# Delta rule and maxout layer on one core: y to DRAM in four transfers, PSUM in two pools, two steps moved

## The chip, the cores and the metric

The kernel runs on one core of one Trainium2 chip. Its time is the device time of one execution, in microseconds (us). TensorE (PE) multiplies matrices and writes to PSUM only; VectorE (DVE), ScalarE (ACT) and GpSimd (POOL) do the elementwise work; SyncE (SP) issues most of the DMA transfers. Each engine takes its own instructions in order, and an engine waits for another one by semaphores.

## The reference

Two layers follow each other. The first is a delta rule over a sequence: for each of 4 batches and 8 heads, with 768 steps of 48 dimensions, in float32. The second is a maxout layer over the 3072 rows that come out of it.

```python
k_n = k / (np.linalg.norm(k, axis=-1, keepdims=True) + 1e-06)
state = 0                                  # (B, H, 48, 48)
for t in range(768):
    y[:, :, t] = einsum('bhd,bhde->bhe', q[:, :, t], state)
    v_old = einsum('bhde,bhd->bhe', state, k_n[:, :, t])
    state += beta_t * einsum('bhd,bhe->bhde', k_n[:, :, t], v[:, :, t] - v_old)
x = y.transpose(0, 2, 1, 3).reshape(3072, 384)
h = maximum(maximum(x @ w1, x @ w2), x @ w3)      # 384 -> 768
out = h @ w_out                                    # 768 -> 384
```

## The kernel before

The sequence is cut into 12 chunks of 64 steps. A chunk is held as two units `g` of two batches each, on 128 partitions. Two chunks of all four batches make a group: 6 groups of 512 rows. For each group the recurrence makes x (in the kernel `xt`, with dimensions on the partitions), and the maxout layer of that group, the generator `ffn(m)`, runs on TensorE while VectorE and ScalarE prepare the recurrence of group m + 1. The order is written out by hand: `ffn(m)` yields after each product of a block, and after the i-th yield the table `LINKS` (or `FOURTH_LINKS` for m = 3 and `LAST_LINKS` for m = 4) names the steps of the next group that are issued there. `STEPS` says how many steps of the triangular solve follow. Within an engine the instructions stand in that order.

The steps that the change and the prediction speak of, by the letters of the tables:

- `g` (`gram`): k k' and k q' of a chunk's batches into `p_g`. DVE masks the q part (`pt`, L401), ACT copies the k part (`at`, L434), and SP sends `at` to DRAM (`at_d`, L447), four transfers for each of two units.
- `blocks`: reads them back as blocks (`x_bl`, L494). `solve` begins with a root on ACT (L272), some small DVE work (L273 to L549), and then 31 steps of two DVE instructions each (L563, L567). Its result goes through DRAM (`y_d`) into `ut`.
- `k`, `q`, `u`, `s`, `y`: products with the state (`p_k`, `p_q`), the solved values (`p_u`), the new state (`p_s`), the result y (`p_y`, added on DVE at L817).
- `x`, `w`, `X`: `y_blocks` (L853) sends y to DRAM (`y_x`), `read_y` (L864) reads it back in another order into `qall`, and `turn_y` (L875) transposes it in 32 x 32 blocks on DVE into `xt`.
- `V` loads values, and `P`, `p` (`prep_values`) scale them: from chunk 10 on DVE, L298.
- `K` loads keys of later units.

In `ffn`, `hidden` multiplies a block of 128 columns of a weight with `xt` into `p_h` (L1221, three matmuls, each shown as two). From m = 1 on, w2 - w1 and w3 - w1 stand in place of w2 and w3: the first gets a relu on ACT (L1231), the second a maximum on DVE (L1235), and what w1 gives is added behind, through w1 times w_out.

The output products of the groups m = 3 to 5 (`outputs`, L988) are done with seven products of halves in place of eight, and the hidden products of m = 5 too (`crossed_hidden`, L1164, six units of eight PSUM tiles each). The sums and differences of the weights that this needs are made by `cross_weights` (parts 0 to 2) and `cross_hidden`; those of x and h by DVE (L1017, L1144 to L1147).

PSUM has eight banks. The pool "psum" holds `ps_ffn` (two banks, in rotation: `p_h`, `p_o`) and `ps_two` (three pairs of banks: all else). At m = 5 this pool is closed, and a new one "banks" is opened, in which `ps_ffn` rotates through all eight banks; two tiles "later" are taken first. A new pool's tile waits for the last reader of what lay there. Where a tile of a rotation is asked for again, its first matmul waits for the reader of the one that had the place.

```python
        if m >= GROUPS - 1:
            psum_pool("banks")

            for _ in range(2):
                ps_ffn([128, TOK], "later")
            yield from crossed_hidden(m, hs)
```

Of the kernel before, what the change touches and what calls it, by code (L numbers as in the profile page):

```python
# [9 lines left out]
FP32 = mybir.dt.float32  # L10
# [13 lines left out]
def kernel(  # L24
# [41 lines left out]
    GROUPS = UNITS // 4  # L66
    TOK = 512
# [5 lines left out]
    dram = ctx.enter_context(  # L73
        tc.tile_pool(name="dram", bufs=2, space=bass.MemoryType.DRAM)
    )
    banks = ctx.enter_context(ExitStack())
    pools = []

    def psum_pool(name):
        banks.close()  # L80
        pools.append(
            banks.enter_context(
                tc.tile_pool(name=name, bufs=1, space=bass.MemoryType.PSUM)
            )
        )

    psum_pool("psum")

    def ps_ffn(shape, name):

        one = len(pools) > 1
        return pools[-1].tile(shape, FP32, name=name, tag="ffn", bufs=8 if one else 2)

    def ps_two(name):
        return pools[-1].tile([128, 2, 512], FP32, name=name, tag="two", bufs=3)


    kpad = [const.tile([128, H, DP], FP32, name=f"kpad{i}") for i in range(4)]
# [21 lines left out]
    def rows(bb):  # L120
        return slice(C * bb, C * (bb + 1))
# [70 lines left out]
    for bb in range(2):  # L192
        nc.gpsimd.affine_select(
            out=mask[rows(bb)], in_=mask[rows(bb)], pattern=[[1, C]], base=-1,
# [123 lines left out]
    def square(name):  # L318
        return work.tile([128, H, C], FP32, name=name, tag="square", bufs=17)
# [169 lines left out]
    def blocks(m, queue=nc.sync):  # L489
        if m == 1:  # L490
            xs[m] = in_wo(0)
        else:
            xs[m] = work.tile([128, 2, HB * BL + HB], FP32, name="x_bl", bufs=1)
        queue.dma_start(  # L494
            out=in_rows(xs[m]),
            in_=at_d[m].rearrange("c f b h j i -> (c f b h) j i"),
        )
# [349 lines left out]
    def y_blocks(c):  # L847


        y = yts.pop(c)  # L850
        y_d = yds[c] = dram.tile([32, 2, 4, DM], FP32, name="y_x")
        for g in range(2):
            nc.sync.dma_start(  # L853
                out=y_d[:, g].rearrange("t b x -> b t x"),
                in_=y[:, g].rearrange("p h d -> p (h d)"),
            )

    def read_y(c):
# [269 lines left out]
    def crossed_hidden(m, hs):  # L1128


        xt, vec = xts[m], nc.vector.tensor_tensor
        plus = vec if m == GROUPS - 1 else nc.gpsimd.tensor_tensor
        lo, hi = slice(0, 256), slice(256, 512)
        a11, a12, a13 = (xt[:, t, lo] for t in range(KT))
        a21, a22, a23 = (xt[:, t, hi] for t in range(KT))
        spare = [t.rearrange("p a h d -> p (a h d)") for t in kmore]
        s1, s2, s3, s4 = (spare[0][:, 256 * n : 256 * (n + 1)] for n in range(4))
        parts = [
            work.tile([128, 2, HB * BL + HB], FP32, name=name, bufs=1).rearrange(
                "p s r -> p (s r)"  # L1140
            )
            for name in ("x_bl", "y_bl")
        ]
        vec(out=s3, in0=a11, in1=a21, op=ALU.subtract)  # L1144
        vec(out=s1, in0=a21, in1=a22, op=ALU.add)
        vec(out=s2, in0=s1, in1=a11, op=ALU.subtract)
        vec(out=s4, in0=a12, in1=s2, op=ALU.subtract)  # L1147
        x_sums[m] = s1, s2, s3, s4
        for j in range(FT):
            hs[j] = square("h").rearrange("p h c -> p (h c)")  # L1150
        for unit in range(2 * PAIRS):
            j, i = divmod(unit, 2)
            w = {
                name: t[:, 128 * j : 128 * (j + 1)]
                for name, t in thirds[1 + i].items()
            }
            top, bottom = hs[j], hs[j + PAIRS]
            held = parts[unit % 2]
            m1, m5, m6, m7 = (held[:, 256 * n : 256 * (n + 1)] for n in range(4))
            c11 = spare[1][:, 256 * (unit // 2 % 2) :][:, 0:256]  # L1160

            def times(to, *terms):
                for n, (stays, moves) in enumerate(terms):
                    nc.tensor.matmul(  # L1164
                        to, w[stays], moves, start=(n == 0), stop=(n == len(terms) - 1)
                    )

            def result(h, base, p, spare=None):
                to = h if i == 0 else base if spare is None else spare
                vec(out=to, in0=base, in1=p, op=ALU.add)  # L1170
                if i:
                    nc.vector.scalar_tensor_tensor(
                        out=h, in0=h, scalar=0.0, in1=to, op0=ALU.max, op1=ALU.max
                    )

            def bank(n):
                return ps_ffn([128, TOK], "p_e" if n % 2 else "p_c")[:, 0:256]

            p = bank(0)
            times(p, ("b11", a11))  # L1180
            nc.scalar.copy(m1, p)
            p = bank(1)
            times(p, ("b21", a12), ("c1", a13))
            result(top[:, lo], m1, p, c11)
            p = bank(2)
            times(p, ("t3", s3))
            nc.scalar.copy(m7, p)
            p = bank(3)
            times(p, ("t1", s1))
            nc.scalar.copy(m5, p)  # L1190
            yield
            p = bank(4)
            times(p, ("t2", s2))
            nc.scalar.copy(m6, p)
            plus(out=m6, in0=m6, in1=m1, op=ALU.add)
            plus(out=m1, in0=m6, in1=m5, op=ALU.add)
            plus(out=m7, in0=m7, in1=m6, op=ALU.add)
            plus(out=m5, in0=m5, in1=m7, op=ALU.add)
            p = bank(5)
            times(p, ("c2", a13), ("b22", s4))  # L1200
            result(bottom[:, lo], m1, p)
            p = bank(6)
            times(p, ("t4", a22), ("c1", a23))
            result(top[:, hi], m7, p)
            p = bank(7)
            times(p, ("c2", a23))
            result(bottom[:, hi], m5, p)
            yield

    def ffn(m):  # L1210
# [30 lines left out]
            for f in range(early):  # L1241
                yield from hidden(f, lo, TOK // 2)
        if m >= GROUPS - 1:
            psum_pool("banks")

            for _ in range(2):
                ps_ffn([128, TOK], "later")
            yield from crossed_hidden(m, hs)
            early = FT
        for f in range(early, FT):  # L1250
# [4 lines left out]
        for i in range(4):  # L1255
            cc, g = divmod(i, 2)
# [20 lines left out]
    def some(gen, n):  # L1277
        for _ in range(n):
            if next(gen, gen) is gen:
                break  # L1280
# [74 lines left out]
    for _ in range(2):  # L1355
# [25 lines left out]
    LINKS = {  # L1381
# [3 lines left out]
    }  # L1385
    FOURTH_LINKS = {
        **LINKS, 14: "w1", 15: "X0", 16: "", 17: "", 19: "X1 P0",
        21: "K0 K1 K2 K3",
    }
    LAST_LINKS = {  # L1390
        0: "k0 q0", 6: "p1", 8: "d0 d1 z0 z1", 9: "j0 j1", 10: "u0", 11: "s0 y0",
# [2 lines left out]

    STEPS = {
        GROUPS - 3: {
            8: 1, 9: 2, 10: 3, 11: 3,
            14: 1, 15: 1, 16: 1, 17: 1, 18: 1, 20: 2, 21: 2,
        },
        GROUPS - 2: {0: 2, 1: 3, 2: 3, 3: 3, 4: 3, 5: 3},  # L1400
    }
# [20 lines left out]
        t=turn, K=load_k, L=lambda n: load_blocks(n, nc.sync),  # L1422
        g=lambda n: gram(n, queues=(nc.gpsimd,) * 2 if n in (10, 11) else one_queue),
# [3 lines left out]
    def links(m, names):  # L1427
        for name in names.split():
            f, i = name[0], int(name[1])
            if f in RECURS and m < GROUPS:  # L1430
                RECURS[f](2 * m + i)
            elif f in MADE and m + 1 < GROUPS:
                MADE[f](2 * (m + 1) + i)
            elif f in UNIT and m + 1 < GROUPS:
                UNIT[f](4 * (m + 1) + i)
            elif f == "N" and m + 2 < GROUPS:
                load_blocks(4 * (m + 2) + i)
# [68 lines left out]
    for m in range(1, GROUPS):  # L1506
        for i, _ in enumerate(ffn(m)):
            if i == 0 and m < GROUPS - 2:
                some(solving, 3)
            if m == 1 and i in (2, 5, 8):  # L1510
                both_layers(i // 3)
            if m == GROUPS - 2 and i in (5, 6):
                cross_hidden(i - 4)
            if m == GROUPS - 3 and i in (5, 6, 11):
                cross_weights((5, 6, 11).index(i))
            if m + 2 < GROUPS:
                if i == 6:
                    blocks(m + 2)
                if i == 8:
                    solving = solve(m + 2)  # L1520
            late = {GROUPS - 3: FOURTH_LINKS, GROUPS - 2: LAST_LINKS}
            links(m + 1, late.get(m, LINKS).get(i, ""))
            if m in STEPS:
                some(solving, STEPS[m].get(i, 0))
            elif i > 7:
                some(solving, 3 if i > 8 else 1)
# [29 lines left out]
```

## Time and profile before

| what | value |
|---|---|
| median of three runs | 512.2 us (512.14 to 513.08) |
| the profiled execution | 513.62 us |
| its span, first to last instruction | 511.9 us |
| mean granted TensorE clock | 0.966 |
| y_x: transfers, size of one | 16, 192 KB |
| qall<-y_x: transfers, size, median to landing | 32, 96 KB, 2.6 us |
| out_dram<-o_sb: transfers, size, median to landing | 36, 96 KB, 2.3 us |
| at_d<-at on SP: transfers, size, median to landing | 72, 32 KB, 2.6 us |

How to read the views: "PE p_c L1164 <- DVE up L1017: 2.2, 1, 2.2" in the table of waits means that TensorE's instructions of line 1164 that write `p_c` waited for DVE's work on `up` of line 1017, 2.2 us in total, once, 2.2 us at most. In the chain of waits each row is a start, a duration and what ran. In a timeline a row is start, duration, engine, line, operation, output and inputs with shapes, how many are merged, and in brackets the idle time before it with what ended it. A row of the windows is the stretch, its length, the busy time of PE, PE's weight load, DVE, ACT and POOL with counts, the granted clock, the share of the 16 DMA engines that was busy, and GB/s. All times are us from the start of the span.

### The profile page before, as it was taken

How to read it: one execution, taken by the hardware profiler on the slowest of the kernel's cores; microseconds unless marked ns; L12 is line 12 of the kernel's file. 1: busy time of each engine (PE TensorE's matmuls, PEld its weight loads, DVE VectorE, ACT ScalarE, POOL GpSimd, SP SyncE). 2: the span in 40 equal slices, each digit the busy share in tenths (PEclk: the TensorE clock that was granted, in tenths of full speed). 3: DMA queues.
4: the chain of work that ended last, by engine and by line, in shares of the span. 5: the costliest groups of instructions: out<-in, count | busy, mean ns of one | idle time of the engine just before them, and what ended most of it. 6: DMA issues, size and time to landing. Idle time of an engine off the chain costs nothing.

```text
span 511.9 us, 18651 instructions
## 1 busy us (share of the span) xinstructions
PE 487.2 (95%) x8064; PEld 340.5 (67%) x8064; DVE 359.0 (70%) x835; ACT 168.7 (33%) x320; POOL 187.0 (37%) x311
## 2 busy tenths in 40 slices
PE   7768989999999999999999999999899999989996
PEld 6657778855565565565555565655696457978895
DVE  5887789978996431899562987663999865458752
ACT  5585655785422142200243101252211042112310
POOL 7434462793391935680485680501000020000000
PEclk9765889999999999999999999999999999999999
DMA  8937869765056935353675454924114320330001
GB/s 110 194 64 214 190 143 165 182 187 129 2 129 141 188 53 124 100 129 101 130 149 127 117 126 97 171 41 97 52 49 97 63 65 14 84 93 1 0 17 46
DMA packets 108672, 53.49 MB, mean 104 GB/s; under 512 B 91760, under 2 KB 102416, under 8 KB 108592
## 3 DMA queue, kind: packets, MB, share of 16 engines
q1 hardware_dynamic: 96832, 31.78, 30.7%
q0 software_dynamic: 9216, 19.85, 16.2%
q8 instruction: 63, 1.03, 0.9%
q10 hardware_dynamic: 2544, 0.69, 0.7%
q14 instruction: 17, 0.14, 0.1%
HBM read 39.17 MB, written 13.11 MB: 102 GB/s over the span
## 4 chain that ended last, share of the span: by engine, by line
PE 71%; DVE 11%; DMA 7%; ACT 4%; SPq 3%; issue 3%; POOL 1%; ACTq 0%; DVEq 0%; POOLq 0%
PE p_h L1221 28%; PE p_o L1263 12%; PE p_o L988 6%; PE p_e L1164 3%; PE p_g L417 3%; PE p_c L1164 3%; DMA y_x<-y 2%; PE p_m L908 2%; PE p_u L773 2%; PE p_k L745 2%; DVE tmp L563 2%; PE p_q L745 2%; PE p_y L815 2%; PE p_s L796 2%; PE p_j L728 2%
## 5 line engine op out<-in xcount | busy, mean ns | idle before, releaser
L1221 PE MATMUL p_h<-xt,w_sb 128*128 128x512 f32 (+1 forms) x450 | 188.5, 562 | 3.4 <-DVE h L1235 2.1
L1221 PEld LDWEIGHTS p_h<-xt,w_sb 128*128 128x128 f32 x450 | 83.3, 195 | 72.5 <-issue 61.6
L1235 DVE TENSOR_TENSOR h<-h,p_h 128x512 f32<-128x512 f32 (+1 forms) x42 | 25.5, 606 | 46.4 <-PE p_h L1221 46.2
L567 DVE TENSOR_TENSOR y_bl<-y_bl,tmp 128x31 f32<-128x31 f32 (+20 forms) x139 | 48.5, 349 | 4.8
L563 DVE TENSOR_TENSOR tmp<-x_bl,y_bl 128x31 f32<-128x31 f32 (+20 forms) x139 | 48.9, 352 | 3.9
L1263 PE MATMUL p_o<-wo_sb,h 128*128 128x384 f32 x144 | 48.9, 490 | 0.0
L375 POOL DMA_DIRECT2D turned<-in_q_dram x72 | 39.3, 554 | 5.8 <-POOL turned L370 2.6
L1263 PEld LDWEIGHTS p_o<-wo_sb,h 128*128 128x128 f32 x144 | 26.7, 190 | 17.2
L1231 ACT ACTIVATE h<-p_h 128x512 f32<-128x512 f32 x24 | 14.3, 597 | 69.3 <-PE p_h L1221 67.8
L265 POOL TENSOR_TENSOR w_sb<-mant,up 128x384 int32<-128x384 int32 x18 | 18.8, 1046 | 41.0 <-DVE mant L261 29.0
L417 PEld LDWEIGHTS p_g<-kqt 48*64 48x64 f32 x1216 | 24.1, 138 | 9.2 <-issue 6.2
L417 PE MATMUL p_g<-kqt 48*64 48x64 f32 (+1 forms) x1216 | 27.3, 238 | 0.9 <-ACT kqt L346 0.8
L803 DVE TENSOR_TENSOR st<-st,p_s 48x768 f32<-48x768 f32 (+1 forms) x18 | 17.1, 950 | 14.3 <-PE p_s L796 14.0
L1269 ACT COPY o_sb<-p_o 128x384 f32<-128x384 f32 x12 | 5.8, 479 | 62.7 <-PE p_o L1263 56.6
L600 POOL DMA_DIRECT2D ut<-y_d x4 | 2.6, 653 | 63.3 <-DMA y_d<-y_bl 63.3
L401 DVE TENSOR_TENSOR pt<-p_g,mask 128x512 f32<-128x512 f32 x20 | 13.7, 688 | 15.5 <-PE p_g L417 15.2
L150 POOL DMA_DIRECT2D v_t<-in_v_dram x14 | 11.6, 832 | 34.8 <-PE p_u L773 34.8
L370 POOL MEMSET turned<- 128x96 f32 x18 | 3.3, 192 | 46.5 <-DVE kqt L391 46.5
L773 PEld LDWEIGHTS p_u<-v_t,ut 64*64 64x64 f32 x768 | 13.5, 141 | 9.6 <-issue 7.6
L434 ACT COPY at<-p_g 128x512 f32<-128x512 f32 x22 | 12.8, 584 | 18.9 <-DVE pt L401 16.6
L375 POOL DMA_DIRECT2D turned<-in_k_dram x32 | 17.5, 556 | 1.2 <-POOL turned L370 1.2
L773 PE MATMUL p_u<-v_t,ut 64*64 64x48 f32 x768 | 15.2, 228 | 2.6 <-issue 1.8
(243 smaller groups left out, 918.0 us busy)
## 6 DMA issues: line engine op xcount, KB each, us to landing
w_bits<-in_moe_w_dram SPq DMA_DIRECT2D x9, 384.0 KB, 6.6
w_bits<-in_moe_w_dram POOLq DMA_DIRECT2D x9, 384.0 KB, 5.2
turned<-in_q_dram POOLq DMA_DIRECT2D x72, 48.0 KB, 2.9
out_dram<-o_sb SPq DMA_DIRECT2D x36, 96.0 KB, 2.3
y_x<-y SPq DMA_DIRECT2D x16, 192.0 KB
qall<-y_x SPq DMA_DIRECT2D x32, 96.0 KB, 2.6
v_t<-in_v_dram POOLq DMA_DIRECT2D x14, 192.0 KB, 5.0
at_d<-at SPq DMA_DIRECT2D x72, 32.0 KB, 2.6
```

The source lines that it names most:

```text
L265: nc.gpsimd.tensor_tensor(out=dst.bitcast(I32), in0=mant_v.bitcast(I32), in1=up_v, op=ALU.add)
L375: (queue, nc.gpsimd)[i].dma_start(out=t[p0 : p0 + 32, bb, at : at + NP * 2 * D].rearrange("p (j x) -> p j x", j=NP), in_=(k, q)[i][2 * bb ...
L417: nc.tensor.matmul(p_g[rows(bb ^ (g * i)), par, c0 : c0 + C * (1 + whole)], kq[:, 0], kq if whole else kq[:, i],)
L563: nc.vector.tensor_tensor(out=t_v, in0=row.to_broadcast(t_v.shape), in1=column.to_broadcast(t_v.shape), op=ALU.mult,)
L567: nc.vector.tensor_tensor(out=rest, in0=rest, in1=t_v, op=ALU.subtract)
L745: nc.tensor.matmul(p_b[rows(bb), par, c0 : c0 + D], kqt[g][dims(par), j, bb ^ g, i], st[dims(par), bb ^ g, g, j],)
L773: nc.tensor.matmul(p_v[rows(bb ^ g), g, i], ut[c % NU][rows(bb), g, h], rhs[rows(bb), g, h],)
L988: nc.tensor.matmul(to[:, g], a[j][:, 128 * g : 128 * (g + 1)], b[j], start=(start and g == j == 0), stop=(stop and g == 1 and j == len(a) ...
L1164: nc.tensor.matmul(to, w[stays], moves, start=(n == 0), stop=(n == len(terms) - 1))
L1221: nc.tensor.matmul(p_h, w_sb[i][:, t, f * 128 : (f + 1) * 128], xt[:, t, lo : lo + w], start=(t == 0), stop=(t == KT - 1),)
L1235: nc.vector.tensor_tensor(out=h, in0=h, in1=p_h, op=ALU.max)
L1263: nc.tensor.matmul(p_o, stays, moves, start=(n == 0), stop=(n == len(terms) - 1))
```

## The change

- `y_blocks` writes y with four transfers, one for each block of 32 partitions (both units), in place of two over all 128 partitions (one for each unit).
- PSUM: `ps_ffn` has a pool of its own with two banks for the whole kernel. The six banks of `ps_two` are a second pool "pairs". At m = 5 only that one is closed, and "banks" is opened with six banks. The first six tiles of a unit in `crossed_hidden` come from there, the last two from `ps_ffn`. The output products that follow take `ps_ffn`.
- `cross_weights`, parts 0 and 1: at yields 6 and 7 of m = 3 in place of 5 and 6, and all three parts behind the links of the yield in place of ahead of them.
- m = 3: `X1` at yield 18 in place of 19, `P0` at 21 in place of 19; one solve step at yield 11 in place of 18.

By the order of the built program, on DVE the first two differences (L928, L932) stand behind both masks L401, and the other four (L949, L959) behind the next L1235. One solve step (207 elements) stands ahead of the sums L1017 of m = 3. `v_t` L298 stands behind the last two readers of `p_o` and two more solve steps. TensorE, ACT and POOL keep their order. On SP two y_x issues become four at each of eight places.

```diff
     def ps_ffn(shape, name):
-        one = len(pools) > 1
-        return pools[-1].tile(shape, FP32, name=name, tag="ffn", bufs=8 if one else 2)
+        return psum.tile(shape, FP32, name=name, tag="ffn", bufs=2)

     def ps_two(name):
-        return pools[-1].tile([128, 2, 512], FP32, name=name, tag="two", bufs=3)
+        return pairs.tile([128, 2, 512], FP32, name=name, tag="two", bufs=3)
...
-        for g in range(2):
+        for b in range(4):
             nc.sync.dma_start(
-                out=y_d[:, g].rearrange("t b x -> b t x"),
-                in_=y[:, g].rearrange("p h d -> p (h d)"),
+                out=y_d[:, :, b], in_=y[32 * b : 32 * (b + 1)].rearrange("p g h d -> p g (h d)")
             )
...
     def crossed_hidden(m, hs):
+        banks = upper_pool("banks")
...
             def bank(n):
-                return ps_ffn([128, TOK], "p_e" if n % 2 else "p_c")[:, 0:256]
+                if n > 5:
+                    return ps_ffn([128, TOK], "p_e")[:, 0:256]
+                return banks.tile([128, TOK], FP32, name="p_c", tag="one", bufs=6)[
+                    :, 0:256
+                ]
...
         if m >= GROUPS - 1:
-            psum_pool("banks")
-
-            for _ in range(2):
-                ps_ffn([128, TOK], "later")
             yield from crossed_hidden(m, hs)
...
     FOURTH_LINKS = {
-        **LINKS, 14: "w1", 15: "X0", 16: "", 17: "", 19: "X1 P0",
-        21: "K0 K1 K2 K3",
+        **LINKS, 14: "w1", 15: "X0", 16: "", 17: "", 18: "X1",
+        21: "P0 K0 K1 K2 K3",
     }
...
         GROUPS - 3: {
-            8: 1, 9: 2, 10: 3, 11: 3,
-            14: 1, 15: 1, 16: 1, 17: 1, 18: 1, 20: 2, 21: 2,
+            8: 1, 9: 2, 10: 3, 11: 4,
+            14: 1, 15: 1, 16: 1, 17: 1, 20: 2, 21: 2,
         },
...
-            if m == GROUPS - 3 and i in (5, 6, 11):
-                cross_weights((5, 6, 11).index(i))
...
             links(m + 1, late.get(m, LINKS).get(i, ""))
+            if m == GROUPS - 3 and i in (6, 7, 11):
+                cross_weights((6, 7, 11).index(i))
```

More of the change, by code (lines that the diff above doesn't have):

```diff
@@ L75, with upper_pool @@
     )
[L76 to L84, printed above, removed]
+    psum = ctx.enter_context(
+        tc.tile_pool(name="psum", bufs=1, space=bass.MemoryType.PSUM)
+    )
+    upper = ctx.enter_context(ExitStack())
+    def upper_pool(name):
+        upper.close()
+        return upper.enter_context(
+            tc.tile_pool(name=name, bufs=1, space=bass.MemoryType.PSUM)
         )
-    psum_pool("psum")
+    pairs = upper_pool("pairs")
     def ps_ffn(shape, name):
-        one = len(pools) > 1
-        return pools[-1].tile(shape, FP32, name=name, tag="ffn", bufs=8 if one else 2)
+        return psum.tile(shape, FP32, name=name, tag="ffn", bufs=2)
     def ps_two(name):
-        return pools[-1].tile([128, 2, 512], FP32, name=name, tag="two", bufs=3)
+        return pairs.tile([128, 2, 512], FP32, name=name, tag="two", bufs=3)
     kpad = [const.tile([128, H, DP], FP32, name=f"kpad{i}") for i in range(4)]
```

## The prediction

> **What bounds the kernel now.** I read the page's busy line first, then TensorE's waits, then the chain of waits around each of the three that lie late, then the timelines there.
>
> ```profile
> PE 487.2 (95%) x8064; PEld 340.5 (67%) x8064; DVE 359.0 (70%) x835; ACT 168.7 (33%) x320; POOL 187.0 (37%) x311
> ```
>
> PE is busy for 487.2 of 511.9 us, so what can be won without removing matmuls is its idle time. TensorE's waits give three entries that the edits can reach (the others lie before 160 us):
>
> ```profile
> PE p_c L1164 <- DVE up L1017: 2.2, 1, 2.2
> PE p_h L1221 <- DVE h L1235: 2.1, 1, 2.1
> PE p_h L1221 <- DVE o_sb L1017: 0.7, 1, 0.7
> ```
>
> By the timeline they stand at 362.10 (2.12 us), 389.75 (0.74) and 457.23 (2.18): 5.04 us in all, and between them PE runs on. The first, by the chain of waits:
>
> ```profile
> 346.43 5.27 DMA at_d<-at
> 351.89 4.98 DMA x_bl<-at_d
> 356.90 0.27 ACT root_bl L272
> 360.22 1.22 DVE x_bl L549
> ```
>
> PE has finished p_q and is free at 359.98, but its next p_h needs a buffer whose reader, DVE's `h` L1235, is queued behind the solve's opening (L273 to L549), and that waits for x_bl, which came from at_d. Why at_d starts late, in VectorE's timeline:
>
> ```profile
> 339.71 0.69 DVE L1235 TENSOR_TENSOR h<-h,p_h 128x512 f32<-128x512 f32 x1 [3.40 <-PE p_h L1221]
> 340.32 0.75 DVE L928 TENSOR_TENSOR w_sb<-wo_sb 128x576 f32<-128x576 f32 x1
> 341.11 0.76 DVE L932 TENSOR_TENSOR wo_sb<-wo_sb 128x576 f32<-128x576 f32 x1
> 341.78 1.28 DVE L401 TENSOR_TENSOR pt<-p_g,mask 128x512 f32<-128x512 f32 x2
> ```
>
> Two weight differences stand ahead of the masks; the two `at` copies on ACT follow the masks (342.50, 343.10), then eight at_d issues on SP (343.11 to 346.87). The third wait, by the chain:
>
> ```profile
> 444.20 6.12 DMA y_x<-y
> ...
> 452.26 2.68 DMA qall<-y_x
> ...
> 456.20 0.51 DVE o_sb L1017
> 456.70 0.48 DVE up L1017
> 457.23 0.70 PE p_c L1164 x2
> ```
>
> Two things end together here: xt (L875) is ready at 456.20, and p_c may start only when `up`, the last reader in the PSUM pool that is being replaced, has ended (457.18). PE itself is free at 455.04 (last p_o, 453.58 + 1.46).
>
> **Part 1, differences behind the masks.** The same 3.2 us of DVE work move one yield later. The cover: DVE idles 3.70 us before its L1235 at 348.36 and 2.74 before L803 at 351.79. L928 and L932 (1.5 us) would run from 342.4, L949 and L959 (1.65) from 349.0 to 350.7; their reader is p_o at 366. Cost nothing; without that cover it would be 1.65 us ahead of L803. The gain: group 2 has the same steps without differences. There L1235 starts at 267.08 and the `at` copies at 268.80 and 269.77, so 1.72 and 2.69 us after it, against 2.79 and 3.39 here. The first at_d issue comes 1.07 us sooner (342.04), and as the issues are back to back, so does the last. What follows can gain more. In group 2 the pair of v_t loads on POOL (273.19) starts as the at_d issues end, and x_bl is issued 6.35 us after the first at_d (269.41, 275.76). Now v_t starts at 345.81, 1.06 before the at_d issues end, and it takes 8.78 (343.11, 351.89). Moved by 1.07, this group stands as group 2 does: x_bl at about 348.4, landed at 353.4. Then DVE's own order is the bound: L817 ends at 354.70, the solve's opening to the end of L1235 takes 4.78 (357.19 to 361.97), so the buffer is free at 359.5 and PE does not wait. Gain 2.12; lower bound 1.07, if only the issue time counts. I take 2.1, since the twin row is the nearest.
>
> **Part 2, order in the fourth group's outputs.** One solve step (0.74 us, the 207 form) moves ahead of the sums L1017, and `v_t` L298 (0.93) moves behind the readers of p_o. Now DVE does xt L875 (ends 388.31), L298, then `o_sb` (ends 389.70), and PE, free at 389.01, waits 0.74. Without L298 `o_sb` would end at 388.87, so the wait goes. Who waits for L298: L757, which has its other input after p_k; its consumer p_u comes 30 us later. Nothing is late next there. The step costs DVE time ahead of y L817: the solve starts 2.4 us earlier, less 0.74, so y comes about 1.5 us earlier while PE comes 2.1 earlier; y_x must therefore save 0.5 us to keep this gain. SP's order around it is the same.
>
> **Part 3, y in four transfers.** 16 transfers of 192 KB become 32 of 96 KB, 0.57 us of SP each: 1.14 us more issue per chunk, and behind it only read_y waits. The row: y_x takes 6.74 us from first issue to landing (443.60 to 450.34), 7.16 at 375.39. DMA shares, for it and for the stores of o_sb:
>
> ```profile
> 445.00:447.00 2.00, 2.00 (x14) 2.00 (x13) 2.00 (x5) 0.48 (x1) 0.00 (x0) 1.00 0.25 53
> 493.50:494.50 1.00, 1.00 (x8) 1.00 (x7) 1.00 (x3) 0.03 (x1) 0.00 (x0) 1.00 0.52 109
> ```
>
> The next to last number is the share of 16 DMA engines: 0.25, a quarter, for transfers whose DRAM side leads with the 4 blocks of 32 rows; 0.52 for 96 KB stores that lead with 64 rows, which land in a median of 2.3 us. The new transfers lead with 64 rows and 32 partitions. Estimate from those rows: last issue at 3 x 0.57 = 1.7, landing 2.3 to 2.9 later, so 4.0 to 4.6; I take 4.3, a saving of 2.4. Bounds: no saving (6.74), and 9.5, the slowest y_x of the trace (299.38 to 308.90, with the DMA share at 0.59).
> The Trainium skill speaks against splitting ("DMA: Bandwidth & Descriptors", Rules for kernel authors): transfers to different partition halves share the same engines and bring nothing, one large transfer is better. By that rule alone y_x would take 6.74 + 1.14 us and the whole change would come out at about 512.4; no row here shows the new shape.
>
> With 2.4 saved, xt is ready at 453.8, before PE is free.
>
> **Part 4, PSUM.** The six banks of the pairs are made anew and the two ffn banks stay, so the first p_c waits for p_y's reader (443.57), no longer for `up`. With part 3, all 2.18 go. Next are the sums L1144 to L1147, which follow `up` on DVE: 455.65 on, needed by the third product at 456.3, with 0.3 us to spare. With y_x as slow as now, xt at 456.2 decides and 1.0 is left. The price comes at the other end. Before, eight banks rotate and the first p_o takes the bank of the last unit's first product; now it takes the ffn bank of that unit's seventh:
>
> ```profile
> 485.82 1.14 PE L988 MATMUL p_o<-wo_sb,h 128*128 128x192 f32 x6
> ...
> 486.66 0.41 DVE L1170 TENSOR_TENSOR y_bl<-y_bl,p_c 128x256 f32<-128x256 f32 x1
> ```
>
> L1170 frees that bank at 487.07, PE could start at 485.82: a new wait of 1.3 us (0.9 to 1.7 by DVE's 0.4 us steps), with all the rest of PE's work behind it. The eighth's bank is free at 487.86, ahead of its use. Inside the units each bank is reused after eight as before: nothing.
>
> **Sum.** 2.1 + 0.7 + 2.2 - 1.3 = 3.7 us off the profiled span of 511.9 (513.62 as a run, 1.7 around it). That run was 1.4 above the median of 512.2; I take the difference off the median: 508.5.
>
> **Rivals.**
> y_x does not get faster. For: no row has its shape. Then part 2 keeps 0.3 and part 4's gain is 1.0: 2.1 + 0.3 + 1.0 - 1.3 = 2.1, 510.1.
> The at_d chain gains its issue time only. For: v_t still crosses x_bl. 1.07 + 0.74 + 2.18 - 1.3 = 2.7, 509.5.
> Slower: four transfers crowd SP and the DMA queue and y_x lands later. Each us beyond 6.74 costs at both xt's, so 2.1 - 2e; it turns slower from e = 1.0, a y_x of 7.8 us, and at 9.5 us it is 3.4 us slower, 515.6. For: the row at 299. Against: that one ran among other loads, while at 375 and 443 the share is 0.32 and 0.20.
> No change: the small losses add up, y_x at about 7.3 to 8.3 us: 512.2.
>
> **How the numbers follow.** Forecast 0.62 (its own range 507.9 to 509.3), at_d only 0.14, y_x unchanged 0.12, no change 0.05, slower 0.07. A measurement of this kernel can tell some 0.2%, 1.0 us, from no change. Faster 0.88, same 0.05, slower 0.07. The low end is all 5.04 us of waits gone and the new one at 0.9, so 508.1, less 0.5 for the spread of the runs (512.14 to 513.08): 507.6. The high end takes in both faster rivals, with the same spread about the slower of them: 510.8. What is left out is the last two cases, the two faster rivals together (511.2), and tails.
>
> **What would show it.** Right: TensorE's waits lose the three entries and gain one, p_o L988 on DVE y_bl L1170, 1.3 us; the chain's y_x pieces shrink to 3 us or less after the last issue, with a DMA share well over 0.25; x_bl is issued near 348.4. Wrong: p_h still waits over 0.5 us for `h` at 360; the crossed stage still begins on xt or the DMA; or a wait inside that stage.

## The result, and the profile after

The changed kernel takes 508.98 us (median of 13 runs, 505.95 to 511.03); the kernel before took 511.64 beside it (13 runs, 509.79 to 515.04). The ratio is 0.9947 with an interval of 0.9921 to 0.9972, so about 2.7 us less (1.4 to 4.0). The forecast was 508.5. The profiled execution of the changed kernel took 507.8 us, with a span of 506.1 us at a granted clock of 0.969, against 511.9 us at 0.966 before. The two profiles thus differ by 5.8 us, twice what the medians do. This is the main thing to clear up.

The page's busy line of the kernel after:

```profile
PE 484.4 (96%) x8064; PEld 338.0 (67%) x8064; DVE 362.5 (72%) x835; ACT 168.7 (33%) x320; POOL 186.4 (37%) x311
```

TensorE's waits after 130 us, in the kernel after (total, times, longest, in us):

```profile
PE p_o L985 <- DVE y_bl L1169: 1.1, 1, 1.1
PE p_u L771 <- DVE v_t L755: 0.5, 1, 0.5
```

The three entries of before (p_c, and p_h twice) are gone. The new one is the one forecast, the first p_o on the last unit's seventh product; its lines have moved by one to three with the edit. The short wait on v_t stands at about 130 us, far ahead of what the change moves, and comes and goes between executions of both kernels.

SP's timeline after, two stretches (start, duration, queue, line, transfer, number of issues):

```profile
340.35 3.76 SPq L445 DMA_DIRECT2D at_d<-at  x8
345.58 0.34 SPq L492 DMA_DIRECT2D x_bl<-at_d  x1
...
438.98 2.51 SPq L851 DMA_DIRECT2D y_x<-y  x4
443.12 2.53 SPq L861 DMA_DIRECT2D qall<-y_x  x4
```

The four y_x transfers are issued from 438.98, and the reading back, which waits for all of them, starts at 443.12: 4.14 us, where it was 6.74. The windows of the kernel after around it (stretch, length, busy time of PE, PEld, DVE, ACT, POOL with counts, granted clock, DMA share, GB/s):

```profile
440.00:441.00 1.00, 1.00 (x9) 1.00 (x7) 1.00 (x4) 0.29 (x1) 0.00 (x0) 1.00 0.53 125
441.00:442.00 1.00, 1.00 (x9) 1.00 (x8) 1.00 (x3) 0.19 (x1) 0.00 (x0) 1.00 0.70 168
442.00:443.00 1.00, 1.00 (x8) 1.00 (x8) 0.79 (x1) 0.00 (x0) 0.00 (x0) 1.00 0.42 103
```

A share of 0.42 to 0.70 stands where 0.25 stood: the transfers now keep more of the 16 DMA engines at work.

TensorE's timeline after, at the beginning and at the end of the crossed stage:

```profile
448.96 1.46 PE L985 MATMUL p_o<-w_sb,xt 128*128 128x192 f32 x8
450.26 1.46 PE L1163 MATMUL p_c<-xt,w_sb 128*128 128x256 f32 x6
...
477.89 1.03 PE L1163 MATMUL p_e<-xt,w_sb 128*128 128x256 f32 x4
480.05 1.24 PE L985 MATMUL p_o<-wo_sb,h 128*128 128x192 f32 x6 [1.14 <-DVE y_bl L1169]
```

At 450.26 the stage begins with no bracket, so no wait; at 480.05 the new wait of 1.14 stands. It ends as VectorE's timeline has it, with the addition that reads the seventh product's bank (479.58 + 0.41 = 479.99):

```profile
479.58 0.41 DVE L1169 TENSOR_TENSOR y_bl<-y_bl,p_e 128x256 f32<-128x256 f32 x1
480.03 0.42 DVE L1171 SCALAR_TENSOR_TENSOR h<-h,y_bl 128x256 f32<-128x256 f32 x1
```

**A measure that two executions can be compared by.** The last `p_g` products of the fourth group, before and after:

```profile
339.54 2.09 PE L417 MATMUL p_g<-kqt 48*64 48x128 f32 x96
337.84 2.09 PE L415 MATMUL p_g<-kqt 48*64 48x128 f32 x96
```

Of what was changed only the y transfers and pools of earlier groups lie ahead of them, and in these two profiles TensorE, apart from the short wait on v_t that both have, waits for nothing between 130 us and there. In further profiles these products start anywhere from 337.8 to 341.8, the changed kernel itself at 337.84 once and at 341.36 another time. So the part ahead of them moves by some 4 us for no reason of the change. Below, "rest" is the time from that start to the end of the span. It was 172.36 in the profile before (511.9 - 339.54) and 168.26 after. Two of the experiments below, `e3_differences_only` and `e7_y_undone`, were profiled in a disturbed execution, so their rests stand in brackets and are compared with none, and the ratios leave such executions out.

### The profile page after: what moved, and what is told of

It reads as the page before. It is cut to its first block, busy times and chain, and to the rows that moved or that the text cites. A ratio compares the mean times of both kernels' runs of the same rounds, so it can differ in the third digit from the quotient of the medians.

```text
span 506.1 us, 18677 instructions
## 1 busy us (share of the span) xinstructions
PE 484.4 (96%) x8064; PEld 338.0 (67%) x8064; DVE 362.5 (72%) x835; ACT 168.7 (33%) x320; POOL 186.4 (37%) x311
## 4 chain that ended last, share of the span: by engine, by line
PE 82%; DVE 6%; DMA 5%; ACT 2%; issue 1%; SPq 1%; POOL 1%; ACTq 0%; DVEq 0%; POOLq 0%
PE p_h L1224 31%; PE p_o L985 13%; PE p_o L1262 12%; PE p_c L1163 4%; PE p_g L415 3%; PE p_u L771 3%; PE p_m L905 2%; PE p_k L743 2%; PE p_y L813 2%; PE p_q L743 2%; PE p_s L794 2%; PE p_j L726 2%; DMA x_bl<-at_d 1%; DMA qall<-in_q_dram 1%; PE p_e L1163 1%
## 5 line engine op out<-in xcount | busy, mean ns | idle before, releaser
L565 DVE TENSOR_TENSOR y_bl<-y_bl,tmp 128x31 f32<-128x31 f32 (+20 forms) x139 | 50.3, 362 | 4.8
L129 POOL DMA_DIRECT2D kpad<-in_k_dram x24 | 16.4, 691 | 3.0 <-PE p_s L794 3.0
```

The lines of the kernel that those rows point to most:

```text
L565: nc.vector.tensor_tensor(out=rest, in0=rest, in1=t_v, op=ALU.subtract)
```

## The experiments

All timed runs, each against runs of the kernel before that were made beside it; their median is in the third column, and the ratio is what counts. "Rest" is from the one profile of each; the sum of TensorE's waits within that rest stands beside it. The two rests in brackets are those of the executions named above.

| kernel | median us (n) | before beside it | ratio to before | rest | waits in it |
|---|---|---|---|---|---|
| before | 511.64 (13) | | 1 | 172.36 | 5.0 |
| after | 508.98 (13) | 511.64 | 0.9947 [0.9921, 0.9972] | 168.26 | 1.1 |
| e1_y_only | 509.02 (8) | 513.4 | 0.9932 [0.9894, 0.9970] | 168.24 | 1.0 |
| e2_pools_only | 512.99 (10) | 513.4 | 0.9991 [0.9961, 1.0022] | 170.94 | 3.2 |
| e3_differences_only | 510.91 (10) | 513.4 | 0.9951 [0.9917, 0.9986] | (171.52) | 2.6 |
| e6_v_later | 511.52 (10) | 513.4 | 0.9972 [0.9940, 1.0004] | 169.94 | 2.6 |
| e4_early_banks | 508.6 (12) | 512.76 | 0.9915 [0.9885, 0.9944] | 166.79 | 0.2 |
| e5_two_by_rows | 509.67 (12) | 512.76 | 0.9932 [0.9901, 0.9963] | 168.33 | 1.3 |
| e7_y_undone | 513.72 (12) | 512.76 | 0.9992 [0.9956, 1.0028] | (173.41) | 4.2 |
| e11_rows_and_early_banks | 509.07 (12) | 511.97 | 0.9929 [0.9904, 0.9955] | 166.93 | 0 |
| e12_old_order | 508.17 (12) | 512.01 | 0.9925 [0.9896, 0.9953] | 167.3 | 0.4 |
| b2_before_again | 510.86 (1) | 511.97 | | 169.88 | 2.6 |
| b3_before_again | 510.7 (1) | 511.97 | | 170.17 | 2.9 |
| a2_changed_again | 511.27 (1) | 511.97 | | 168.24 | 1.1 |

Rest less waits lies between 166.6 and 167.7 in every row without brackets. What the change does after `p_g` is therefore told by TensorE's waits, to within about a microsecond.

**y in four transfers, alone.** `e1_y_only` is the kernel before with this edit:

```diff
-        for g in range(2):
+        for b in range(4):
             nc.sync.dma_start(
-                out=y_d[:, g].rearrange("t b x -> b t x"),
-                in_=y[:, g].rearrange("p h d -> p (h d)"),
+                out=y_d[:, :, b], in_=y[32 * b : 32 * (b + 1)].rearrange("p g h d -> p g (h d)")
```

> Only y_blocks is changed: four transfers by 32 partitions, pools and order as before. Measured from the start of the fourth group's last p_g products (339.5 us in the profile before) to the end of the span: 172.3 us before, 168.2 with the whole change. Theory 1 (the transfer's shape is what costs, its waits are PE's): y_x takes 4.1 us from first issue to landing in place of 6.7, the wait of p_c L1164 falls from 2.2 to 0.7 (it then waits for the pool's last reader, up, alone), the 2.1 us at p_h stays, 0.5 to 0.7 stays at o_sb; 170.6. Theory 2 (the landing of y is hidden behind the PSUM pool's last reader): p_c still waits about 2 us, 172.

Measured 509.02, ratio 0.9932 [0.9894, 0.9970]. Its TensorE waits:

```profile
PE p_u L773 <- DVE v_t L757: 1.0, 1, 1.0
PE p_c L1163 <- DVE up L1016: 0.6, 1, 0.6
PE p_h L1220 <- DVE o_sb L1016: 0.4, 1, 0.4
```

The wait of p_c falls from over 2 us to 0.6 with the old PSUM pools: `up` itself comes earlier, since it follows xt on VectorE. No wait of p_h for `h` is there, though the differences are where they were. The rest, 168.24, is that of the whole change. As far as rest and ratio can tell, this edit alone is worth all that the change is worth.

**The PSUM pools, alone.** `e2_pools_only` is the changed kernel with the old y transfers and the old order of the fourth group. The core of the edit against before:

```diff
-                return ps_ffn([128, TOK], "p_e" if n % 2 else "p_c")[:, 0:256]
+                if n > 5:
+                    return ps_ffn([128, TOK], "p_e")[:, 0:256]
+                return banks.tile([128, TOK], FP32, name="p_c", tag="one", bufs=6)[
+                    :, 0:256
+                ]
```

> Only the PSUM pools are changed, y in two transfers and the order as before. Theory 1: p_c waits for xt alone, which is ready at the same time as before: its wait falls by 1.0 from 2.2 to 1.2, and p_o gains a wait of 1.1 to 1.3 for the bank of the last unit's seventh product; from the p_g products to the end 172.3 to 172.6, so the pools alone bring nothing. Theory 2 (the pool's last reader was the bound): p_c's wait goes, 2.2 less, with the new wait 171.3.

Measured 512.99, ratio 0.9991 [0.9961, 1.0022]: nothing that can be told from no change. Its waits:

```profile
PE p_c L1164 <- DVE kmore L1144: 1.2, 1, 1.2
PE p_o L986 <- DVE y_bl L1170: 1.1, 1, 1.1
PE p_h L1225 <- DVE o_sb L1015: 0.9, 1, 0.9
PE p_u L771 <- DVE v_t L755: 0.4, 1, 0.4
```

The last is the one at 130 us. With y slow, p_c no longer waits for `up` but 1.2 us for the sums of xt (`kmore`), and the price at the other end, 1.1, takes back the 0.8 to 1.0 that is won.

**The differences behind the masks, alone.** `e3_differences_only` is the kernel before with this edit:

```diff
-            if m == GROUPS - 3 and i in (5, 6, 11):
-                cross_weights((5, 6, 11).index(i))
...
             links(m + 1, late.get(m, LINKS).get(i, ""))
+            if m == GROUPS - 3 and i in (6, 7, 11):
+                cross_weights((6, 7, 11).index(i))
```

> Only cross_weights is moved behind the links and a yield later, all else as before. Theory 1 (at_d then no longer crosses the load of v_t): x_bl is issued 5.2 to 6.4 us after the first at_d in place of 8.8, p_h's 2.1 us wait for h goes, some 0.4 stays at o_sb; from the p_g products to the end 169.9. Theory 2 (only the issue time is gained): x_bl is issued 7.7 us after the first at_d or more, 1.0 of the wait stays, 171.2.

Measured 510.91, ratio 0.9951 [0.9917, 0.9986]. x_bl is issued 5.2 us after the first at_d, as theory 1 has it, and the wait for `h` is not in its profile; the waits left in the rest are p_c on `up`, 2.1, and p_h on `o_sb`, 0.5. The ratio claims some 2.5 us (0.7 to 4.3), and no wait that went can account for more than the 2.1 of the first profile. The comparisons below of two kernels that differ by the order alone don't show that gain, so I do not count it.

**v_t's load out of at_d's way.** `e6_v_later` is the kernel before, with the two loads V0 and V1 of the fourth group behind a copy of one element on POOL that waits for the opened solve's data (it adds this copy):

```diff
-        **LINKS, 14: "w1", 15: "X0", 16: "", 17: "", 19: "X1 P0",
+        **LINKS, 4: "j0 j1 t3", 7: "N1", 10: "k1 q1 V0 V1", 14: "w1", 15: "X0", 16: "", 17: "", 19: "X1 P0",
...
+            if m == GROUPS - 3 and i == 10:
+                nc.gpsimd.tensor_copy(small("pause", 1), in_rows(xs[m + 2])[:, 0, 0:1])
```

> The differences stay where they were; instead the two loads of values of the fourth group's yields (V0, V1) are issued behind a 1-element copy on POOL that waits for the opened solve, so that they can't cross at_d. Theory 1 (v_t's packets are what delays at_d): x_bl is issued about 5.5 us after the first at_d in place of 8.8, p_h's 2.1 us wait for h is gone though the masks are as late as before; from the p_g products to the end about 170.0. Theory 2 (the late start of at_d is all): x_bl is issued 8.8 us after, the wait stays 2.1, 172.3.

Measured 511.52, ratio 0.9972 [0.9940, 1.0004]. x_bl was issued 7.2 us after the first at_d, not 5.5. SP's wait for at_d ahead of x_bl, in this run, in `b2_before_again` below and in the changed kernel:

```profile
SPq L494 <- DMA at_d<-at: 3.2, 1, 3.2
SPq L494 <- DMA at_d<-at: 4.0, 1, 4.0
SPq L492 <- DMA at_d<-at: 1.2, 1, 1.2
```

From the start of `p_g` x_bl was issued after 10.76, 11.64 and 7.74 us. So v_t's load costs at_d some 0.9 us here, and taking it away does not bring what the new order brings. The rest is in the trace's packet records. The landing of the eight at_d transfers is marked by 128 packets of 4 bytes. In `e6_v_later` all but one are there by 347.1; the last comes at 348.62, behind 16 data packets that start at 348.33, just as a packet of 16 KB of the DMA queue named `instruction` ends (347.42 to 348.34). In the profiles with the old order the last mark comes 0.7 to 1.9 us after the one before it; with the new order, where at_d is over before v_t's packets and the next packet of that queue begin, 0.03 at most. The records don't say which DMA engine carries a packet, so that the 16 packets stood behind the one of 16 KB is inferred from the times. The wait for `h` was absent here as well, so this run could not tell whether the crossing made it.

**The kernel before, twice more, and the changed one once more.** By now the wait of 2.1 us for `h` had shown in one profile alone. These three are the same two kernels again, with a profile each.

> The kernel before, unchanged, profiled once more. Theory 1 (the 2.1 us wait of p_h for h belongs to this order): the wait is there again, x_bl takes about 5 us from its issue to the root on ACT, 172.3 from the p_g products to the end. Theory 2 (x_bl landed late in that one execution, as three kernels with the masks as late as before suggest): x_bl takes about 3.5 us, no wait at p_h for h, 170.2.

> As the one before it: a third profile of the kernel before. Theory 1: wait of 2.1 us at p_h. Theory 2: no wait, x_bl about 3.5 us, 170.2 from the p_g products to the end.

> The changed kernel, unchanged, profiled once more: if its waits after 160 us are a matter of the order, the same single wait of 1.1 us at p_o and 168.2 to 168.4 from the p_g products to the end; the part ahead of it may differ by some us, as the spans of all kernels do.

Measured 510.86 and 510.7 for the kernel before, 511.27 for the changed one. The waits of `b2_before_again`, and there is no third:

```profile
PE p_c L1164 <- DVE up L1017: 2.0, 1, 2.0
PE p_h L1221 <- DVE o_sb L1017: 0.6, 1, 0.6
```

`b3_before_again` has 2.0 and 0.9 and the wait on v_t, 0.7. So the kernel before has the wait for `h` in one of three profiles; among all seven profiles with the differences in the old place (e1, e2, e12 and, with v_t's load moved, e6 are the others) it is in that one alone. What was different is in ScalarE's timeline, in the bracket of the root that opens the solve. The kernel before as first profiled:

```profile
356.90 0.26 ACT L272 ACTIVATE root_bl<-x_bl 128x32 f32<-128x32 f32 x1 [4.50 <-DMA x_bl<-at_d]
```

And `b2_before_again`:

```profile
354.50 0.26 ACT L272 ACTIVATE root_bl<-x_bl 128x32 f32<-128x32 f32 x1 [2.33 <-DMA x_bl<-at_d]
```

From the issue of x_bl to the root it is 5.0 us in the first and 3.5 us in the second. For comparison the root in the kernel after, 6.3 us from the issue:

```profile
351.84 0.26 ACT L270 ACTIVATE root_bl<-x_bl 128x32 f32<-128x32 f32 x1 [1.14 <-DMA x_bl<-at_d]
```

The windows of the kernel before as first profiled, just ahead of the root:

```profile
354.54:355.54 1.00, 1.00 (x3) 0.41 (x3) 0.17 (x1) 0.00 (x0) 0.00 (x0) 1.00 0.15 49
355.54:356.54 1.00, 1.00 (x4) 0.40 (x3) 0.00 (x0) 0.00 (x0) 0.00 (x0) 1.00 0.15 18
```

And of `b2_before_again`:

```profile
352.96:353.96 1.00, 1.00 (x4) 0.48 (x3) 0.97 (x2) 0.00 (x0) 0.00 (x0) 1.00 0.81 311
353.96:354.96 1.00, 1.00 (x3) 0.38 (x2) 0.70 (x2) 0.26 (x1) 0.00 (x0) 1.00 0.01 4
```

In `b2_before_again` the transfer runs at a share of 0.81 and is over. In the first profile two more microseconds follow with a share of 0.15, and VectorE has nearly nothing to do. Little of that share is x_bl's. By the packet records its 128 packets of 4 KB have ended by 355.12 and 15 of the 16 marks of its landing by 355.13; from 355.95 on the packets of 1536 bytes of the y_x issued at 354.74 run. Between 354.82 and 355.94 the DMA view of the first profile counts, by queue:

```profile
q8 instruction: 1, 0.02, 5.2%
q1 hardware_dynamic: 3, 0.00, 1.1%
```

The three of q1 are x_bl's last data packet (354.97) and its last two marks, at 355.12 and 355.77. The one of the instruction queue has 16 KB and runs from 354.86 to 355.79, and the last mark comes as it ends. In `b2_before_again` such a packet runs from 353.92 to 354.86, and all of x_bl's marks are over by 354.14: none stood behind it. So one mark that fell behind a packet of instructions, and not ahead of it, held the whole solve. That both used the same DMA engine is again inferred from the times. It explains 0.65 us of the 1.5; the semaphore then changed only at 356.87, 1.1 us after the mark, where the mark before it took 0.35, and why isn't known. It was one execution's accident, and the forecast had priced it as the kernel's habit.

With that, the change's steady effect is read from the rests: 169.88 and 170.17 before, 168.26 and 168.24 after, so 1.8 us. It lies inside the timed interval of 1.4 to 4.0.

**Another pair of banks.** `e4_early_banks` is the changed kernel with the third and fourth product of a unit, not the seventh and eighth, in the two ffn banks that p_o takes next:

```diff
-                if n > 5:
+                if n in (2, 3):
```

> The whole change, but in each unit of crossed_hidden the third and fourth product take the two ffn banks and the seventh and eighth the new pool, so that the first p_o asks for a bank that ACT has read long before. Theory 1 (rotation is what makes the new wait): p_o's 1.1 us wait for y_bl goes and nothing comes in its place; from the p_g products to the end 167.1 in place of 168.2, the time 1.1 us below the whole change. Theory 2 (DVE is the bound at that place, h is late anyway): p_o waits as long for h, 168.2.

Measured 508.6, ratio 0.9915 [0.9885, 0.9944]; rest 166.79, against 168.26. TensorE's timeline at the end of the crossed stage:

```profile
480.05 1.03 PE L1163 MATMUL p_c<-xt,w_sb 128*128 128x256 f32 x4
480.91 1.14 PE L985 MATMUL p_o<-wo_sb,h 128*128 128x192 f32 x6
```

The first p_o follows the last product with no wait. The price of part 4 is shown to come from the bank that the next stage inherits, and it can be avoided at no cost. This is the best version by its rest and its ratio, though its interval overlaps that of the changed kernel: the timed runs do not separate 1.1 us.

**Two transfers, but led by rows.** `e5_two_by_rows` is the changed kernel with two transfers by unit, as before, of which each runs over all 128 partitions into a `y_x` that is laid out as [4, 32, 2, ...]; the reading back is rearranged to match (not shown):

```diff
-        y_d = yds[c] = dram.tile([32, 2, 4, DM], FP32, name="y_x")
-        for b in range(4):
+        y_d = yds[c] = dram.tile([4, 32, 2, DM], FP32, name="y_x")
+        for g in range(2):
             nc.sync.dma_start(
-                out=y_d[:, :, b], in_=y[32 * b : 32 * (b + 1)].rearrange("p g h d -> p g (h d)")
+                out=y_d[:, :, g].rearrange("b t x -> (b t) x"),
+                in_=y[:, g].rearrange("p h d -> p (h d)"),
```

> The whole change, but y goes out in two transfers of 128 partitions whose DRAM side leads with 128 rows (the DRAM tile is laid out by block, row, unit), and the read takes the same 384-byte pieces from there. Theory 1 (the shape of the old transfers cost, not their number): y_x lands 3.0 to 3.6 us after the first issue, DMA share over 0.5 while it runs; from the p_g products to the end 168.2, as there is slack already. Theory 2 (four transfers in flight are what is fast): y_x takes 6 us or more, p_c waits 1 us again, 169.3.

Measured 509.67, ratio 0.9932 [0.9901, 0.9963]. SP's timeline:

```profile
441.01 0.99 SPq L851 DMA_DIRECT2D y_x<-y  x2
443.76 2.53 SPq L862 DMA_DIRECT2D qall<-y_x  x4
```

And the window while the two run:

```profile
442.00:443.00 1.00, 1.00 (x8) 1.00 (x7) 1.00 (x4) 0.26 (x1) 0.00 (x0) 1.00 0.87 319
```

Two transfers of the old size land in 2.75 us, sooner than the four smaller ones, at a share of 0.87. So it was the shape of the old ones that was slow, the leading 4 on their DRAM side, not their number or size; nor was it the layout of `y_x`, which e1 keeps. The trace has a direct sign of it: the semaphore of a y_x transfer changes 5 times for each of the 16 old ones, and 16 times for each of the 16 of this run and for 31 of the 32 of the changed kernel. The further 1.4 us bring nothing, since xt is early enough already: the rest is 168.33, and p_o's wait of 1.1 is there.

**Without the new y.** `e7_y_undone` is the changed kernel with the two old transfers back (the reverse of e1's edit).

> The whole change with y in two transfers as before. Theory 1: xt is late by 6.7 - 4.1 = 2.6 us against the whole change, of which 1.3 is slack (449.1 to 450.4 in its profile): p_c waits 1.2 us, and 0.3 to 0.5 comes back at the first p_h of the fifth group; from the p_g products to the end 169.7 to 169.9 in place of 168.2. Theory 2 (y is hidden): 168.2.

Measured 513.72, ratio 0.9992 [0.9956, 1.0028]: all the rest of the change together, pools and order, brings nothing by itself that can be told from no change. Next to `e2_pools_only` (0.9991), from which it differs by the moved order alone, it also shows no gain from that order, though each of the two intervals leaves some 2 us open to either side. In its bracketed profile p_c waits 1.2 us, as expected, but the other wait is not the 0.3 to 0.5 that was expected:

```profile
PE p_h L1225 <- DVE o_sb L1015: 1.9, 1, 1.9
```

VectorE, which works in order, stands 3.1 us at the transposition into xt until qall lands, and `o_sb` is queued behind it. With y slow, the moved order makes this wait longer (e2 has 0.9).

**The two improvements together.** `e11_rows_and_early_banks` has the edits of e4 and of e5.

> Early banks (third and fourth product in the ffn banks) and y in two transfers that lead with 128 rows, on top of the changed kernel. Theory 1 (both late waits and p_o's are gone already with early banks; y lands 1.7 us sooner than needed): no wait over 0.3 us after 160 us, 166.8 from the p_g products to the end as with early banks alone, time as there within what can be told. Theory 2 (y's landing still paces something): 0.5 us or more below early banks alone.

Measured 509.07, ratio 0.9929 [0.9904, 0.9955]; rest 166.93 against 166.79 of e4. A faster y_x is worth no more once TensorE no longer waits for what depends on it: no wait is left in the rest (the one after 130 us is that on v_t, 1.0, ahead of it).

**The old order with the best pools.** `e12_old_order` is e4 with the differences, P0, X1 and the solve steps of m = 3 where they were before:

```diff
-        **LINKS, 14: "w1", 15: "X0", 16: "", 17: "", 18: "X1",
-        21: "P0 K0 K1 K2 K3",
+        **LINKS, 14: "w1", 15: "X0", 16: "", 17: "", 19: "X1 P0",
+        21: "K0 K1 K2 K3",
...
+            if m == GROUPS - 3 and i in (5, 6, 11):
+                cross_weights((5, 6, 11).index(i))
...
-            if m == GROUPS - 3 and i in (6, 7, 11):
-                cross_weights((6, 7, 11).index(i))
```

> Early banks and y in four transfers, but the order of the fourth group as in the kernel before (differences, X1, P0 and the solve step back). Theory 1 (the order brings only part 2's wait, as x_bl lands in time anyway): the 0.4 us at o_sb of the kernel with y alone is back and nothing else; from the p_g products to the end 167.2 in place of 166.8. Theory 2 (the moved differences matter in most executions): p_h waits 2 us for h, 169 or more.

Measured 508.17, ratio 0.9925 [0.9896, 0.9953]; rest 167.3. Its waits:

```profile
PE p_h L1224 <- DVE o_sb L1014: 0.4, 1, 0.4
PE p_u L771 <- DVE v_t L755: 0.4, 1, 0.4
```

The one wait that the old order brings back is that for `o_sb`, 0.4 (that on v_t is the one at 130 us). That is what the moved order is worth by waits and rest; the timed runs don't show it (508.17 against e4's 508.6, ratios 0.9925 and 0.9915).

## Why the prediction was right, point by point

The sign, the time and the three lost waits came as forecast, but the sum behind them has one term too many.

**Part 1: x_bl moved as forecast, the term was mis-sized.** The step "Gain 2.12; lower bound 1.07 ... I take 2.1" failed. The first half came about: the first at_d is issued 1.06 us sooner after `p_g` (2.51 in place of 3.57; 1.07 was forecast), and x_bl 5.2 us after the first at_d (345.58 - 340.35), where 6.35 was estimated and it was 8.8 before; from the start of `p_g`, 7.7 us in place of 11.6. The forecast's reason, v_t's load, is only part of these 3.9 us: 1.1 is issue time, e6 gives v_t 0.9, and of the other 2.0 e6 shows 1.5 in the lag of at_d's last mark, which the forecast didn't know. Then x_bl takes 6.3 us from its issue to the root (6.3 to 6.8 in the profiles with the new order, those in brackets left out) where it took 3.3 to 3.6 with the old one, but for the accident. It now runs beside v_t's load, which POOL issues at 344.12, and its last mark comes 1.0 to 1.7 us after the fifteenth. That v_t's load is the reason is argued; no run has the new order and that load elsewhere. So the root comes only about a microsecond earlier (14.0 to 14.6 us after the start of `p_g` in place of 15.0 to 15.4). On the clock of the first profile, 1.70 us later, that is at 353.5, where 353.4 was forecast, so in that one execution the wait would have gone. In the others that microsecond meets no wait of TensorE: the 2.1 us were there in one of seven profiles with the old order. The rival of the at_d chain, with its 1.07, allowed for less gain but shared the mistake. Measured value: 0 as a rule.

**Part 2: right, at about its size, as long as y is fast.** The wait for `o_sb` is gone. It is 0.6 and 0.9 in the repeats of the kernel before (forecast 0.74), and 0.4 once y is fast (e1, e12). The forecast said that y_x must save 0.5 us to keep this gain; with y slow (e7) the wait is 1.9, where its rival of a slow y_x still kept a gain of 0.3.

**Part 3: right.** 4.14 us against 4.3, for the reason that was given. The Trainium skill ("DMA: Bandwidth & Descriptors", Rules for kernel authors) advises against splitting by partitions; that advice did not decide here, as the one transfer was not spread over all engines in the first place. The same page (Why a DMA increments its semaphore by 16 and not by 1) states that a transfer uses the largest number of engines, up to 16, that divides the slowest dimension of each of its sides. The shares agree: 0.25 with a leading 4, and 0.87 with 128 on both sides; so do the changes of the semaphores, 5 and 16.

**Part 4: right at both ends.** p_c's wait goes from 2.0 (b2, b3) to nothing, and p_o's wait is 1.14 where 1.3 was forecast. With y slow the wait that is left is 1.2 on xt's sums, the case in which the forecast left 1.0 of gain (e2: 0.8). What it did not say is that most of the 2.2 belongs to y: with y alone 0.6 is left. So, y being fast, the pools win 0.6 and lose 1.1. With e4's choice they lose nothing (166.79 against 168.26); that no new pools at all would be better too, by about 0.5, follows from these numbers but was not run.

**The sum.** Taken from typical executions: 0 + 0.7 + 2.0 - 1.1 = 1.6, against 1.8 by the rests and 2.7 (1.4 to 4.0) by the timed runs; the forecast had 3.7. The 1.0 by which it was above the timed gain was half made up by its base, 512.2 of three runs, for which 13 runs gave 511.64; so 508.5 came within 0.5 of 508.98. That closeness is partly luck: one term stood for an accident, and the base leaned the other way. Two of the forecast's bounds don't come out of their own terms, without effect on the rest: 510.1 and half a spread of 0.5 give 510.6, not 510.8, and the two faster rivals together give 511.1, not 511.2. The difference of the two profiles, 5.8, holds 1.7 from the part ahead of `p_g` (339.54 - 337.84) and 4.1 from the rest, of which about 2.3 is the late x_bl (172.36 less the mean of 169.88 and 170.17).

**Left open.** Why the last mark of x_bl, once it was through, took another 1.1 us in the first profile. Why e3 measured 0.9951, more than its waits explain, while two pairs of kernels that differ by the order (e7 and e2, e4 and e12) show no such gain. And what moves the part ahead of `p_g` by 4 us from one execution to another. Most of it arises in the first quarter: in the profiles without brackets the 2501st of the 8064 matmuls starts anywhere from 121.8 to 125.6 us, and from there to `p_g` it is 215.5 to 217.6. The granted clock there differs between executions (20 to 40 us: 0.67 in the first profile before, 0.52 in that after; from 100 us on 1.00 in both), but no run shows it to be the cause.

## What to carry to other kernels

Before a wait is priced, see whether it is there in a second and a third execution: a transfer that ran late once looks in one profile just like a queue that is ordered badly. Where the last few packets of a transfer come late, look at what other queues moved just then, the instruction queue too. For a transfer that lands late at a low share of the DMA engines, look at the outermost dimension of both its sides before its size or its place. When a PSUM pool is split, give the next stage the banks whose readers are done first.

## What was not expected of the hardware

The changed kernel begins its fourth group's `p_g` products at 337.84 us in one execution and at 341.36 in another, while the 168 to 170 us that follow repeat to within 0.3 for the same kernel (169.88 and 170.17; 168.26 and 168.24), but for the one late x_bl. One packet of 16 KB of the instruction queue takes 0.9 to 1.5 us (0.93 in the first profile, where a mark of 4 bytes came only as it ended). And an x_bl of 3.5 us takes 6.3 in the new order, with v_t's load beside it, so a transfer that is issued 4 us sooner may land only 1 us sooner.
